# GateLoop and squared ReLU on one core: the inverse of the running products taken from 1/|a| and from each block's product, and idle products in every planned TensorE stop

## The chip, the core and the metric

The kernel runs on one core of one Trainium2 chip. A core has five engines that work side by side, each through its own queue in order: TensorE (PE) multiplies matrices into PSUM, VectorE (DVE) and ScalarE (ACT) do elementwise work, GpSimd (POOL) and SyncE (SP) here mostly issue DMA transfers. The metric is the device time of one execution in microseconds (us). The kernel before takes 721.93 us, the median of three runs (720.88 to 722.63).

## The reference

A gated linear recurrence with complex gates, for 4 batches, 8 heads, 768 positions and head size 48, followed by a two-layer block with squared ReLU on 3072 tokens (384 to 2048 to 384). All is fp32.

```python
mag = np.sqrt(a_re * a_re + a_im * a_im)
scale = np.minimum(mag, 0.999) / (mag + 1e-06)
a_re_n, a_im_n = (a_re * scale, a_im * scale)
for t in range(S):
    ar, ai = (a_re_n[:, :, t, :, None], a_im_n[:, :, t, :, None])
    new_re = ar * S_re - ai * S_im
    new_im = ar * S_im + ai * S_re
    kv = np.einsum('bhd,bhe->bhde', k[:, :, t], v[:, :, t])
    S_re, S_im = (new_re + kv, new_im)
    y[:, :, t] = np.einsum('bhd,bhde->bhe', q[:, :, t], S_re)
# y is regrouped to x: (B*S, H*D)
h = x @ w_in
r = np.maximum(h, 0.0)
out = (r * r) @ w_out
```

## The kernel before

The tokens are cut into six units of 512 (`n` = 0 to 5). Within a unit, partition p holds four consecutive steps (`c` = 0 to 3) of all eight heads, in two halves of four heads (`z` = 0, 1). A tile with one value per step, head and channel of a half is 128 x 768 fp32. A batch has 768 steps, so unit 1 and unit 4 cross from one batch to the next (`cross`), and units 2 and 5 end with a batch (`ends`).

Instead of stepping, the kernel multiplies queries by the running product of the gates and keys by its inverse, and then uses masked products of queries and keys. The inverse of a complex number is its conjugate over its squared size, so what is needed is one over the squared size of each running product. This is what the change touches. Per unit:

- `chain(n)`: `roots` computes 1/|a| (Ln, Exp with -0.5, one Newton step) into slot 3 (`t`) of the four slots `col[z]` of the buffer `f`. `normalise` makes from it the normalised gates: f0 = 0.999 t, f1 = 1 - 1e-6 t, gate times min(f0, 1) f1 (L938 to L945). `inner` forms the running products over the four steps in a partition (L964 to L972) and copies the last ones, the blocks' own products, to `xn[:, 0:2]` (L979). `totals`, `scan` and `back` form the running products over the 128 partitions: a turn on TensorE (L1023), small complex products on VectorE, a turn back, a copy by ACT (L1217). After `back`, `xn[:, 0:2]` is the running product ahead of each block.
- `inverse(z)`: squares of the running products in the partition (L984), their sum (L986), Ln (L988), Exp with -1 (L990) and a Newton step (L992, L994) give one over the squared size of all 768 values; the last of each four goes to `xn[:, 2]` (L999).
- `factors(lo, hi, rk)`: the same inverse for the products ahead of the blocks, by a running product of the blocks' inverses: TensorE turns `xn[:, 2]` (L1071), `scan_x` on VectorE runs six scans of 64 (L1092), starting from a small constant or from the value kept of the unit before (`cx`), and writes two checks of range (`grow`, L1096, and `total`, L1100); TensorE turns back (L1114), ACT copies (L1117). Unit 0 does it in two parts, one for each z.
- `twist(z)` multiplies the keys by the inverses in the partition (L1004). `apply(z, p, np)` multiplies the gates' running products by `xn[:, 0:2]` (L1255, L1259), the keys by `xn[:, 2]` (L1262), and queries and keys by the result (L1269). It uses the slots of `f` as its own buffers; from unit 2 on it does four heads at once, L1255's second half into slots 2 and 3.
- `gather` sends slices of the keys between partitions by DMA (L1309, to `KC`). `pairs(n)` turns queries and keys (`turn_pe` on TensorE in units 0 and 1, L1368 and L1372; `turn` by VectorE and DMA afterwards), forms scores (L1386), masks them (L1389), updates the state (L1414 to L1425) and mixes (L1438, L1442); ACT copies the output to `yt` (L1448) and a DMA takes it to `xT` (L1456).
- `dense(n, grp)` multiplies `xT` by the first weights (L1478), ACT squares the ReLU (L1509, L1510), and TensorE multiplies by the second weights (L1524 in unit 0, L1575 in `eight` and `seven` after that).

The weights arrive once, as 64-bit floats, and are converted in pieces on ACT and VectorE (L805 to L818) during units 0 and 1. `check` steps sum squares of inputs on ACT (L948, L952, L1228, L1231) into `sums`; `verdict` compares them, and a flag chooses a general path if they leave the range.

No order is written out by hand. Each helper hands a step (engine, estimated duration, what it reads and writes, a rank) to `Plan.add`. `Plan.order` builds the order of all engines by simulating them with these estimates: of the steps that are ready on an engine, it takes the one of the lowest rank, then the oldest. To a TensorE step's wait for another engine after 100 us it adds a margin of 0.6 us, and of 2.0 us where scores and state products wait for transfers. If TensorE stands for more than `FILL` = 1.0 us before a step, and the planned time is under `UNTIL` = 100 us, `Plan.emit` puts idle products ahead of it, `(stop - 0.3) / 0.22` of them: products of the identity with itself into bank `d2` (L711), read by nobody. The eight PSUM banks are `d0` to `d2` (dense products; in unit 0 `turn_pe` uses the first two), `sc0`, `sc1`, `tr0`, `tr1` (turns; in unit 1 `turn_pe`), and `yp`.

Of the kernel before, what the change touches and what calls it, by code (L numbers as in the profile page):

```python
# [480 lines left out]
class Plan:  # L481
# [7 lines left out]
    FILL, EACH, UNTIL = 1.0, 0.22, 100.0  # L489

    def __init__(self, idle):
        self.idle = idle
        self.steps = []
        self.wrote = {}
        self.read = {}

    def add(self, eng, dur, reads, writes, fn, rank, wire=None, group=None, after=(), slack=False):

        n = len(self.steps)
        deps = set(after)  # L500
# [18 lines left out]
    def order(self):  # L519
# [30 lines left out]
        for _ in steps:  # L550
# [46 lines left out]
def fast_path(ctx, tc, q, k, v, a_re, a_im, moe_w_in, moe_w_out, out, flag):  # L597
# [6 lines left out]
    C = 128  # L604
# [13 lines left out]
    CUT = C // 2  # L618
# [32 lines left out]
    x = sb("x", NM * (C + 1)).rearrange("p (m c) -> p m c", m=NM)  # L651
    xe = sb("xe", NM)
    txs = [sb(f"tx{j}", 3 * 24).rearrange("p (r g) -> p r g", r=3) for j in range(2)]
    ce = sb("ce", 2 * NM).rearrange("p (r m) -> p r m", r=2)
    cx = sb("cx", NM)
# [16 lines left out]
    NS = 10  # L672
    sums = sb("sums", NU * NS).rearrange("p (n j) -> p n j", n=NU)
    grow = sb("grow", NU * 2 * NM).rearrange("p (n j m) -> p n j m", n=NU, j=2)
    total = sb("total", B * NM).rearrange("p (b m) -> p b m", b=B)
# [27 lines left out]
    for t in txs:  # L703
        pool.memset(t, 0.0)
    pool.memset(good, 1.0)
    pool.memset(col, 1.0)
# [4 lines left out]
    plan = Plan(lambda: pe.matmul(bank["d2"][:, 0:C], lhsT=ident, rhs=ident, start=True,  # L711
                                  stop=True))
# [176 lines left out]
    def chain(n):  # L889
# [46 lines left out]
        def normalise(z):  # L936
            f0, f1, _, t = col[z]
            step("ACT", ac(Y), key(z, 3), key(z, 0), lambda: act.activation(  # L938
                out=f0, in_=t, func=AF.Copy, scale=0.999), first)
            step("ACT", ac(Y), key(z, 3), key(z, 1), lambda: act.activation(  # L940
                out=f1, in_=t, func=AF.Copy, scale=-1e-6, bias=1.0), first)
# [9 lines left out]
            if n == 0:  # L951
                check("ACT", ac(Y), key(z, 2), [], lambda: act.activation(  # L952
                    out=junk[:, 0:Y], in_=col[z][2], func=AF.Copy, saturate=False,
                    accum_out=sums[:, n, z:z + 1]), first)
# [26 lines left out]
        def inverse(z):  # L981
            f0, f1, d, t = col[z]
            rk = late[z]
            step("ACT", ac(Z), [("a", z)], key(z, 0, 1), lambda: act.activation(  # L984
                out=ff[z][:, 0:Z], in_=A[z], func=AF.Square), rk)
            step("DVE", tt(Y), key(z, 0, 1), key(z, 2), lambda: dve.tensor_tensor(  # L986
                out=d, in0=f0, in1=f1, op=ALU.add), rk)
            step("ACT", ac(Y), key(z, 2), key(z, 0), lambda: act.activation(  # L988
                out=f0, in_=d, func=AF.Ln), rk)
            step("ACT", ac(Y), key(z, 0), key(z, 1), lambda: act.activation(  # L990
                out=f1, in_=f0, func=AF.Exp, scale=-1.0), rk)
            step("DVE", tt(Y), key(z, 1, 2), key(z, 3), lambda: dve.scalar_tensor_tensor(  # L992
                out=t, in0=d, scalar=-1.0, in1=f1, op0=ALU.mult, op1=ALU.mult), rk)
# [767 lines left out]
```

## Time and profile before

| | us |
|---|---|
| median of three runs | 721.93 |
| profiled execution, whole | 722.42 |
| its span, first to last instruction | 720.6 |
| TensorE busy | 698.5 (97%) |
| VectorE busy | 576.5 (80%) |
| ScalarE busy | 358.7 (50%) |
| GpSimd busy | 176.3 (24%) |
| idle products L711 among TensorE's | 64.0, 530 records |
| TensorE's last product ends at | 713.9 |

A busy TensorE is not a useful one: the records of idle products count too. Each fp32 product leaves two records. Records of matmuls overlap, so the pace of a stream is read from the chain of waits (when a stretch starts and how long it takes), not from the mean of a record. A share of busy time is a mean over stages with different limits, so the stages are looked at one by one.

### The profile page before, as it was taken

How to read it: one execution, taken by the hardware profiler on the slowest of the kernel's cores; microseconds unless marked ns; L12 is line 12 of the kernel's file. 1: busy time of each engine (PE TensorE's matmuls, PEld its weight loads, DVE VectorE, ACT ScalarE, POOL GpSimd, SP SyncE). 2: the span in 40 equal slices, each digit the busy share in tenths (PEclk: the TensorE clock that was granted, in tenths of full speed). 3: DMA queues.
4: the chain of work that ended last, by engine and by line, in shares of the span. 5: the costliest groups of instructions: out<-in, count | busy, mean ns of one | idle time of the engine just before them, and what ended most of it. 6: DMA issues, size and time to landing. Idle time of an engine off the chain costs nothing.

```text
span 720.6 us, 12695 instructions
## 1 busy us (share of the span) xinstructions
PE 698.5 (97%) x4648; PEld 633.5 (88%) x4648; DVE 576.5 (80%) x1188; ACT 358.7 (50%) x579; POOL 176.3 (24%) x333
## 2 busy tenths in 40 slices
PE   9999889999988999999999999999999999999996
PEld 9998778677767898999999898998998989999995
DVE  6999999799777599889799588999788997347521
ACT  6693557975465713447713659324479142122230
POOL 6504253052400003314026040033050033032100
PEclk9999899999998999999999999999999999999998
DMA  9742359230530003645007671017560045197400
GB/s 284 213 161 53 79 117 288 81 66 18 162 107 23 1 12 98 176 112 155 1 25 200 158 150 40 0 55 196 136 162 4 10 122 132 47 356 238 152 2 26
DMA packets 56360, 79.60 MB, mean 110 GB/s; under 512 B 10944, under 2 KB 38464, under 8 KB 56288
## 3 DMA queue, kind: packets, MB, share of 16 engines
q0 software_dynamic: 15232, 40.72, 18.7%
q1 hardware_dynamic: 36928, 32.98, 18.0%
q10 hardware_dynamic: 4128, 4.98, 2.6%
q8 instruction: 39, 0.64, 0.4%
q14 instruction: 33, 0.27, 0.1%
HBM read 48.76 MB, written 4.72 MB: 74 GB/s over the span
## 4 chain that ended last, share of the span: by engine, by line
PE 81%; DVE 10%; ACT 3%; DMA 2%; SPq 1%; issue 1%; POOL 0%; DVEq 0%; ACTq 0%; POOLq 0%
PE d L1478 29%; PE d L1575 26%; PE d L711 7%; PE sc L1386 5%; PE d L1524 4%; PE tr L1414 3%; PE yp L1438 2%; PE yp L1442 2%; DVE f L964 2%; PE tr L1023 1%; DMA KC<-f 1%; SPq L1309 1%; DVE w L818 1%; PE tr L1071 1%; DVE aq L945 1%
## 5 line engine op out<-in xcount | busy, mean ns | idle before, releaser
L1478 PE MATMUL d<-xT,w 128*128 128x256 f32 x1056 | 236.2, 381 | 1.0 <-DMA xT<-yt 1.0
L1478 PEld LDWEIGHTS d<-xT,w 128*128 128x128 f32 x1056 | 199.2, 191 | 27.6 <-issue 1.1
L1575 PE MATMUL d<-w,g 128*128 128x192 f32 x768 | 132.3, 327 | 0.0
L1575 PEld LDWEIGHTS d<-w,g 128*128 128x128 f32 x768 | 124.9, 190 | 1.0 <-issue 0.7
L1509 ACT ACTIVATE g<-d 128x512 f32<-128x512 f32 x88 | 52.4, 595 | 127.5 <-PE d L1478 111.0
L1309 POOL DMA_DIRECT2D KC<-f x160 | 78.9, 501 | 117.2 <-DVE f L1269 55.9
L1590 DVE TENSOR_TENSOR g<-g 128x512 f32<-128x512 f32 x64 | 43.7, 689 | 37.1 <-ACT g L1510 21.5
L885 POOL DMA_DIRECT2D v<-in_v_dram x80 | 46.7, 590 | 86.5 <-PE yp L1438 30.3
L1575 PE MATMUL d<-T,g 128*128 128x192 f32 x384 | 66.8, 326 | 0.0
L711 PE MATMUL d<-ident 128*128 128x128 f32 x530 | 64.0, 283 | 1.5 <-POOL ident masks.py:199 1.5
L711 PEld LDWEIGHTS d<-ident 128*128 128x128 f32 x530 | 62.7, 199 | 1.8 <-POOL ident masks.py:199 1.5
L1575 PEld LDWEIGHTS d<-T,g 128*128 128x128 f32 x384 | 62.9, 190 | 0.0
L1536 POOL DMA_DIRECT2D out_dram<-ot x22 | 12.4, 563 | 206.4 <-DVE ot L1599 136.5
L1510 ACT ACTIVATE g<-g 128x512 f32<-128x512 f32 x96 | 60.6, 631 | 3.0
L1386 PE MATMUL sc<-QT 96*128 96x128 f32 x368 | 49.8, 291 | 4.2 <-ACT QT L1372 3.3
L1386 PEld LDWEIGHTS sc<-QT 96*128 96x128 f32 x368 | 46.0, 202 | 7.2 <-ACT QT L1372 4.1
L1269 DVE TENSOR_TENSOR f<-aq 128x384 f32<-128x384 f32 (+1 forms) x64 | 45.0, 752 | 0.6
L1255 DVE TENSOR_TENSOR f<-aq,xn 128x384 f32<-128x384 f32 (+1 forms) x64 | 44.7, 748 | 0.0
L1524 PE MATMUL d<-w,g 128*128 128x384 f32 x128 | 43.3, 488 | 0.7 <-DVE w L818 0.7
L1599 DVE TENSOR_TENSOR ot<-ot,d 128x192 f32<-128x192 f32 x64 | 21.7, 349 | 21.6 <-PE d L1575 21.1
L1448 ACT COPY yt<-yp 112x512 f32<-112x512 f32 x24 | 26.2, 1092 | 23.4 <-PE yp L1442 23.4
L964 DVE TENSOR_TENSOR f<-aq 128x384 f32<-128x384 f32 x72 | 36.9, 554 | 0.9
(196 smaller groups left out, 1029.7 us busy)
## 6 DMA issues: line engine op xcount, KB each, us to landing
QT<-aq SPq DMA_DIRECT2D x128, 64.0 KB, 2.0
f<-in_moe_w_in_dram POOLq DMA_DIRECT2D x8, 768.0 KB, 7.1
f<-in_moe_w_out_dram POOLq DMA_DIRECT2D x8, 768.0 KB, 5.9
KC<-f POOLq DMA_DIRECT2D x104, 48.0 KB, 2.6
out_dram<-ot POOLq DMA_DIRECT2D x22, 192.0 KB, 2.2
QT<-aq ACTq DMA_DIRECT2D x64, 64.0 KB, 2.3
v<-in_v_dram POOLq DMA_DIRECT2D x80, 48.0 KB, 2.9
xT<-yt SPq DMA_DIRECT2D x36, 96.0 KB, 2.4
```

What stands on the lines that cost most here:

```text
L711: plan = Plan(lambda: pe.matmul(bank["d2"][:, 0:C], lhsT=ident, rhs=ident, start=True, stop=True))
L885: lambda i=i, c=c, src=src: pool.dma_start(out=t[32 * c:32 * c + 32, i], in_=src[c]), vrank, 32 * 1536, 4.0,
L964: dve.tensor_tensor(out=f, in0=a[:, :, :, c - 1], in1=a[:, j, :, c].unsqueeze(1).to_broadcast([C, 2, HH, D]), op=ALU.mult)
L1255: lambda j=j, r=r: dve.tensor_tensor(out=f4[:, j, r], in0=a[:, r], in1=over(j), op=ALU.mult), late[z])
L1269: lambda j=j, r=r, o=o: dve.tensor_tensor(out=o[:, :, :, r * D:(r + 1) * D], in0=qk[:, j], in1=a[:, r], op=ALU.mult), late[z])
L1309: lambda i=i, c=c, queue=queue: queue.dma_start(out=kc[32 * c:32 * c + 32, i], in_=nat[32 * i:32 * i + 32, c]),
L1386: pe.matmul(sa[:, j], lhsT=T[:, j, 1, h], rhs=T[:, j, 0, h], start=True, stop=True)
L1478: pe.matmul(ps, lhsT=w1[:, f // FP, m, ts(f % FP, C)], rhs=xT[:, n % 2, m, ts(grp, G)], start=(m == 0), stop=(m == NM - 1))
L1509: act.activation(out=o, in_=ps, func=AF.Relu)
L1510: act.activation(out=o, in_=o, func=AF.Square)
L1524: pe.matmul(ps, lhsT=gt[:, f % 2, ts(i, C)], rhs=w2[:, f], start=(f == 0), stop=(f == NF - 1))
L1575: pe.matmul(bank[b][:, 0:DH], lhsT=g4[:, r, j], rhs=w(j), start=first and j == 0, stop=last and j == NT - 1)
```

## The change

`inverse` no longer squares the running products. In `normalise`, f1 is now made in two steps, f2 = 1 + 1e-6 t into slot 2 and f1 = 2 - f2; slot 2 is kept. `inverse` takes max(t, 1/0.999) times f2 for each single step, squares it, and multiplies along the four steps in the partition, three products of 192 elements for each half. The result stays in slot 2, where `twist` reads it. The unit-0 sum over slot 2 moves ahead of f2, which overwrites that slot.

`factors` is called once for a unit, with both halves, and takes the products ahead of the blocks, `xn[:, 0:2]`, after `back`: squares, a sum, a scaling where the sum is under 1, Ln, Exp with -1, a Newton step, all on 128 x 384, into `xn[:, 2]`. The turns, the scans and the carried value are gone. In units that cross or end a batch, two products of 192 and a sum on ACT write a new column of `sums`. A step `edges` squares 24 values of each part of `xn` for the check of range, which `verdict` evaluates.

In the planner, idle products fill stops over 0.8 us at any time, into a bank of `d2`, `d1`, `d0` that is free by the plan. `turn_pe` in unit 0 takes all three d banks in turn.

```diff
-    FILL, EACH, UNTIL = 1.0, 0.22, 100.0
-
-    def __init__(self, idle):
+    FILL, EACH = 0.8, 0.22
+
+    def __init__(self, idle, banks):
         self.idle = idle
+        self.lives = {b: [[]] for b in banks}
...
+        for k in {*reads, *writes}:
+            if k[0] in self.lives:
+                self.lives[k[0]][-1].append(n)
...
                 stop = t - free[e]
-                if t < self.UNTIL and stop > self.FILL:
-                    self.fill[n] = int((stop - 0.3) / self.EACH)
+                spare = [b for b in self.lives if self.spare(b, done, free[e])]
+                if spare and stop > self.FILL:
+                    self.fill[n] = int((stop - 0.3) / self.EACH), spare[0]
...
+    def spare(self, b, done, t):
+
+        return all(all(done.get(n, 1e9) < t - 0.5 for n in life) or not any(n in done for n in life)
+                   for life in self.lives[b])
+
     def emit(self):
         for n in self.order():
-            for _ in range(self.fill.get(n, 0)):
-                self.idle()
+            many, b = self.fill.get(n, (0, None))
+            for _ in range(many):
+                self.idle(b)
...
         def normalise(z):
-            f0, f1, _, t = col[z]
+            f0, f1, f2, t = col[z]
             step("ACT", ac(Y), key(z, 3), key(z, 0), lambda: act.activation(
                 out=f0, in_=t, func=AF.Copy, scale=0.999), first)
-            step("ACT", ac(Y), key(z, 3), key(z, 1), lambda: act.activation(
-                out=f1, in_=t, func=AF.Copy, scale=-1e-6, bias=1.0), first)
+            if n == 0:
+                check("ACT", ac(Y), key(z, 2), [], lambda: act.activation(
+                    out=junk[:, 0:Y], in_=f2, func=AF.Copy, saturate=False,
+                    accum_out=sums[:, n, z:z + 1]), first)
+
+            step("ACT", ac(Y), key(z, 3), key(z, 2), lambda: act.activation(
+                out=f2, in_=t, func=AF.Copy, scale=1e-6, bias=1.0), first)
+            step("ACT", ac(Y), key(z, 2), key(z, 1), lambda: act.activation(
+                out=f1, in_=f2, func=AF.Copy, scale=-1.0, bias=2.0), first)
             step("DVE", tt(Y), key(z, 0, 1), key(z, 0), lambda: dve.scalar_tensor_tensor(
                 out=f0, in0=f0, scalar=1.0, in1=f1, op0=ALU.min, op1=ALU.mult), first)
...
         def inverse(z):
-            f0, f1, d, t = col[z]
+
+
+            _, _, f2, t = col[z]
             rk = late[z]
-            step("ACT", ac(Z), [("a", z)], key(z, 0, 1), lambda: act.activation(
-                out=ff[z][:, 0:Z], in_=A[z], func=AF.Square), rk)
-            step("DVE", tt(Y), key(z, 0, 1), key(z, 2), lambda: dve.tensor_tensor(
-                out=d, in0=f0, in1=f1, op=ALU.add), rk)
-            step("ACT", ac(Y), key(z, 2), key(z, 0), lambda: act.activation(
-                out=f0, in_=d, func=AF.Ln), rk)
-            step("ACT", ac(Y), key(z, 0), key(z, 1), lambda: act.activation(
-                out=f1, in_=f0, func=AF.Exp, scale=-1.0), rk)
-            step("DVE", tt(Y), key(z, 1, 2), key(z, 3), lambda: dve.scalar_tensor_tensor(
-                out=t, in0=d, scalar=-1.0, in1=f1, op0=ALU.mult, op1=ALU.mult), rk)
-            step("DVE", tt(Y), key(z, 1, 3), key(z, 3), lambda: dve.scalar_tensor_tensor(
-                out=t, in0=t, scalar=2.0, in1=f1, op0=ALU.add, op1=ALU.mult), rk)
-            xh = xn.rearrange("p r (h d) -> p r h d", h=H)[:, :, ts(z, HH)]
-            t4 = t.rearrange("p (h c d) -> p h c d", h=HH, c=W)
-            step("ACT", ac(Y // W), key(z, 3), third(z * HH * D, (z + 1) * HH * D),
-                 lambda: act.copy(out=xh[:, 2], in_=t4[:, :, W - 1]), rk)
+            step("DVE", tt(Y), key(z, 2, 3), key(z, 2), lambda: dve.scalar_tensor_tensor(
+                out=f2, in0=t, scalar=1.0 / 0.999, in1=f2, op0=ALU.max, op1=ALU.mult), rk)
+            step("ACT", ac(Y), key(z, 2), key(z, 2), lambda: act.activation(
+                out=f2, in_=f2, func=AF.Square), rk)
+            t4 = f2.rearrange("p (h c d) -> p h c d", h=HH, c=W)
+            for c in range(1, W):
+                step("DVE", tt(Y // W), key(z, 2), key(z, 2), lambda c=c: dve.tensor_tensor(
+                    out=t4[:, :, c], in0=t4[:, :, c - 1], in1=t4[:, :, c], op=ALU.mult), rk)
 
         def twist(z):
-            t = col[z][3]
+            t = col[z][2]
             kk = QK[z][:, Y:2 * Y]
-            step("DVE", tt(Y), key(z, 3) + [("qk", z)], [("k", z)], lambda: dve.tensor_tensor(
+            step("DVE", tt(Y), key(z, 2) + [("qk", z)], [("k", z)], lambda: dve.tensor_tensor(
                 out=kk, in0=kk, in1=t, op=ALU.mult), late[z])
...
-        def factors(lo, hi, rk):
-
-            rows = [(m, max(lo - C * m, 0), min(hi - C * m, C)) for m in range(lo // C, (hi - 1) // C + 1)]
-            ks = third(lo, hi)
-            b = trs[slot["tr"] % 2]
-            ps = bank[b][:, 0:DM].rearrange("p (m t) -> p m t", m=NM)
-            slot["tr"] += 2
-
-            def go():
-                for m, p0, p1 in rows:
-                    pe.matmul(ps[p0:p1, m], lhsT=xn[:, 2, C * m + p0:C * m + p1], rhs=ident,
-                              start=True, stop=True)
-            step("PE", 0.12 * len(rows), ks, [(b,)], go, rk)
-
-            groups = [([m for m, p0, p1 in rows if (p0, p1) == (0, C)], 0, C)] + [
-                ([m], p0, p1) for m, p0, p1 in rows if (p0, p1) != (0, C)]
-
-            def scan_x():
-                for ms, p0, p1 in groups:
-                    if not ms:
-                        continue
-                    sl = slice(ms[0], ms[-1] + 1)
-                    if fresh:
-                        dve.memset(x[p0:p1, sl, 0], SCALE ** -2)
-                    else:
-                        dve.tensor_copy(out=x[p0:p1, sl, 0], in_=cx[p0:p1, sl])
-                    for hf in range(2):
-                        t0, t1 = hf * CUT, (hf + 1) * CUT
-                        if hf and cross:
-                            dve.memset(x[p0:p1, sl, t0], SCALE ** -2)
-                        for m in ms:
-                            dve.tensor_tensor_scan(
-                                out=x[p0:p1, m, t0 + 1:t1 + 1], data0=ps[p0:p1, m, t0:t1],
-                                data1=mask[p0:p1, 0:CUT], initial=x[p0:p1, m, t0:t0 + 1],
-                                op0=ALU.mult, op1=ALU.bypass)
-                        dve.scalar_tensor_tensor(
-                            out=grow[p0:p1, n, hf, sl], in0=x[p0:p1, sl, t0], scalar=2.0 ** 124,
-                            in1=x[p0:p1, sl, t1], op0=ALU.mult, op1=ALU.is_ge)
-                        if (ends and hf) or (cross and not hf):
-                            dve.tensor_scalar(
-                                out=total[p0:p1, ps_[0][2], sl], in0=x[p0:p1, sl, t1],
-                                scalar1=2.0 ** 114, scalar2=None, op0=ALU.is_le)
-                    if not ends:
-                        dve.tensor_copy(out=cx[p0:p1, sl], in_=x[p0:p1, sl, C])
-            kx = [("x", i) for _, _, i in ks]
-            check("DVE", sum(0.5 + 0.6 * len(ms) for ms, _, _ in groups if ms), [(b,)] + kx, kx,
-                  scan_x, rk)
-
-            b2 = trs[(slot["tr"] + 1) % 2]
-            ps2 = bank[b2][:, 0:DM]
-
-            def go2():
-                for m, p0, p1 in rows:
-                    pe.matmul(ps2[:, C * m + p0:C * m + p1], lhsT=x[p0:p1, m, 0:C],
-                              rhs=ident[p0:p1, p0:p1], start=True, stop=True)
-            step("PE", 0.12 * len(rows), kx, [(b2,)], go2, rk)
-            step("ACT", ac(hi - lo), [(b2,)], ks, lambda: act.copy(
-                out=xn[:, 2, lo:hi], in_=ps2[:, lo:hi]), rk)
+        def factors(rk):
+
+            X = [("xn", 2, i) for i in range(6)]
+            e0, e1, d = (e[:, j].rearrange("p w g -> p (w g)") for j in range(3))
+            f = x[:, 0:DM]
+            step("ACT", ac(2 * DM), [("xn", j, z) for j in range(2) for z in range(2)], E,
+                 lambda: act.activation(out=e[:, 0:2].rearrange("p r w g -> p r (w g)"),
+                                        in_=xn[:, 0:2], func=AF.Square), rk)
+
+            def scaled():
+
+                dve.tensor_tensor(out=d, in0=e0, in1=e1, op=ALU.add)
+                dve.tensor_scalar(out=f, in0=d, scalar1=1.0, scalar2=2.0 ** 59,
+                                  op0=ALU.is_lt, op1=ALU.mult)
+                dve.scalar_tensor_tensor(out=d, in0=f, scalar=2.0 ** -59, in1=d,
+                                         op0=ALU.max, op1=ALU.mult)
+            step("DVE", 2 * tt(DM) + ts2(DM), E, E + [("x",)], scaled, rk)
+            step("ACT", ac(DM), E, E, lambda: act.activation(out=e0, in_=d, func=AF.Ln), rk)
+            step("ACT", ac(DM), E, E, lambda: act.activation(
+                out=e0, in_=e0, func=AF.Exp, scale=-1.0), rk)
+
+            def refined():
+                dve.scalar_tensor_tensor(out=e1, in0=d, scalar=-1.0, in1=e0,
+                                         op0=ALU.mult, op1=ALU.mult)
+                dve.scalar_tensor_tensor(out=e1, in0=e1, scalar=2.0, in1=e0,
+                                         op0=ALU.add, op1=ALU.mult)
+                dve.scalar_tensor_tensor(out=xn[:, 2], in0=f, scalar=2.0 ** -59, in1=e1,
+                                         op0=ALU.max, op1=ALU.mult)
+            step("DVE", 3 * tt(DM), E + [("x",)], E + X, refined, rk)
+            if not ends and not cross:
+                return
+
+            for z in range(2):
+                t3 = col[z][2].rearrange("p (h c d) -> p h c d", h=HH, c=W)[:, :, W - 1]
+                step("DVE", tt(Y // W), key(z, 2) + X, [("x",)], lambda z=z, t3=t3:
+                     dve.tensor_tensor(
+                         out=x[:, ts(z, DM // 2)].rearrange("p (h d) -> p h d", h=HH),
+                         in0=t3, in1=xn[:, 2, ts(z, DM // 2)].rearrange(
+                             "p (h d) -> p h d", h=HH), op=ALU.mult), rk)
+            check("ACT", ac(DM), [("x",)], [], lambda: act.activation(
+                out=junk[:, 0:DM], in_=x[:, 0:DM], func=AF.Copy, saturate=False,
+                accum_out=sums[:, n, NS - 1:NS]), rk)
...
+        def edges(r):
+            blocks = xn[:, r].rearrange("p (g b) -> p g b", b=32)[:, :, ::31]
+            check("ACT", 0.2, [("xn", r, 0), ("xn", r, 1)], [], lambda: act.activation(
+                out=ends_of[:, n, r], in_=blocks, func=AF.Square), ahead)
...
+            edges(j)
...
-            factors(zs[0] * HH * D, (zs[-1] + 1) * HH * D, late[zs[0]])
+            if 0 in zs:
+                factors(rank)
...
+        if kind == "d":
+            plan.lives["d%d" % (s % n)].append([])
...
-                b = "d%d" % (take("d0", 2)) if n == 0 else trs[take("tr", 2)]
+                b = "d%d" % take("d", 3) if n == 0 else trs[take("tr", 2)]
...
-            for lo, hi, top_ in ((0, 2, 60), (2, 4, 12), (4, NS, 20)):
+            for lo, hi, top_ in ((0, 2, 60), (2, 4, 12), (4, NS - 1, 20), (NS - 1, NS, 114)):
...
-            dve.tensor_reduce(out=good[:, 1:2], in_=grow, axis=AXYZ, op=ALU.min)
-            dve.tensor_reduce(out=good[:, 2:3], in_=total, axis=AXY, op=ALU.min)
+            for b in range(2):
+                dve.tensor_tensor(out=ends_of[:, :, 0, :, b], in0=ends_of[:, :, 0, :, b],
+                                  in1=ends_of[:, :, 1, :, b], op=ALU.add)
+            grow = ends_of[:, :, 1, :, 0]
+            dve.scalar_tensor_tensor(out=grow, in0=ends_of[:, :, 0, :, 0], scalar=2.0 ** -124,
+                                     in1=ends_of[:, :, 0, :, 1], op0=ALU.mult, op1=ALU.is_le)
+            dve.tensor_reduce(out=good[:, 1:2], in_=grow, axis=AXY, op=ALU.min)
```

More of the change, by code (lines that the diff above doesn't have):

```diff
@@ L617, in fast_path @@
     G = L // 2
-    CUT = C // 2
     Z = 2 * HH * W * D
@@ L650, in fast_path @@
     el = sb("el", 3 * NM).rearrange("p (r m) -> p r m", r=3)
-    x = sb("x", NM * (C + 1)).rearrange("p (m c) -> p m c", m=NM)
-    xe = sb("xe", NM)
+    x = sb("x", DM)
     txs = [sb(f"tx{j}", 3 * 24).rearrange("p (r g) -> p r g", r=3) for j in range(2)]
     ce = sb("ce", 2 * NM).rearrange("p (r m) -> p r m", r=2)
-    cx = sb("cx", NM)
     xn = sb("xn", 3 * DM).rearrange("p (r n) -> p r n", r=3)
@@ L671, in fast_path @@
     mask = sb("mask", C)
-    NS = 10
+    NS = 11
     sums = sb("sums", NU * NS).rearrange("p (n j) -> p n j", n=NU)
-    grow = sb("grow", NU * 2 * NM).rearrange("p (n j m) -> p n j m", n=NU, j=2)
-    total = sb("total", B * NM).rearrange("p (b m) -> p b m", b=B)
+    ends_of = sb("ends_of", NU * 2 * NM * W * 2).rearrange("p (n r g b) -> p n r g b", n=NU,
+                                                           r=2, b=2)
     odd = sb("odd", NF)
@@ L705, in fast_path @@
     pool.memset(good, 1.0)
+    pool.memset(sums, 0.0)
     pool.memset(col, 1.0)
@@ L708, in fast_path @@
     pool.memset(txs[1].rearrange("p r (m k) -> p r m k", k=4)[:, 0, :, 0], 1.0)
-    plan = Plan(lambda: pe.matmul(bank["d2"][:, 0:C], lhsT=ident, rhs=ident, start=True,
-                                  stop=True))
+    plan = Plan(lambda b: pe.matmul(bank[b][:, 0:C], lhsT=ident, rhs=ident, start=True,
+                                    stop=True), ["d2", "d1", "d0"])
     def vs(n):
@@ L950, in normalise @@
                 accum_out=sums[:, n, 2 + z:3 + z]), first)
[L951 to L954, printed above, removed]
         def inner(z):
@@ L981, in inverse @@
         def inverse(z):
[L982 removed]
+            _, _, f2, t = col[z]
             rk = late[z]
[L984 to L999 removed]
+            step("DVE", tt(Y), key(z, 2, 3), key(z, 2), lambda: dve.scalar_tensor_tensor(
[6 more added lines that the diff above has]
+                    out=t4[:, :, c], in0=t4[:, :, c - 1], in1=t4[:, :, c], op=ALU.mult), rk)
         def twist(z):
[L1002 removed]
+            t = col[z][2]
             kk = QK[z][:, Y:2 * Y]
[L1004 removed]
+            step("DVE", tt(Y), key(z, 2) + [("qk", z)], [("k", z)], lambda: dve.tensor_tensor(
                 out=kk, in0=kk, in1=t, op=ALU.mult), late[z])
+        E = [("e", 0), ("e", 1), ("e", 2)]
         for fn in (roots, normalise, inner):
@@ L1142, in minus @@
             dve.tensor_scalar(out=ni, in0=im, scalar1=-1.0, scalar2=None, op0=ALU.mult)
-        E = [("e", 0), ("e", 1), ("e", 2)]
         I = [("yt", 0), ("yt", 1)]
@@ L1311, in gather @@
                     rank, 32 * w * 4, group=(n, p))
-    slot = {"d0": 0, "tr": 0, "sc": 0, "A": 0, "St": 0, "yt": 0, "QT": 0, "d": 0, "ot": 0, "g": 0}
+    slot = {"tr": 0, "sc": 0, "A": 0, "St": 0, "yt": 0, "QT": 0, "d": 0, "ot": 0, "g": 0}
     trs = ["tr0", "tr1"]
@@ L1666, in verdict @@
         ps = bank["tr0"][0:1, 0:1]
-        step("DVE", 2.2, [], [("good",)], collect, (LATE, 99), after=checked)
+        step("DVE", 2.6, [], [("good",)], collect, (LATE, 99), after=checked)
         step("PE", 0.3, [("good",)], [("tr0",)], lambda: pe.matmul(
```

## The prediction

> **What bounds the kernel now.** I read the slices first, then a table of busy time by stage, the chain of waits, the groups of instructions by shape, and the timeline where these left a question. All times are of the profiled execution: span 720.6 us, whole run 722.42 us, so 1.8 us lie around the span. The median of the runs is 721.93, half a microsecond lower. A difference under 0.2% (1.4 us) can't be told from none.
>
> The slices show TensorE near full throughout, but its clock below full in two slices before the last, and VectorE near full until slice 10:
>
> ```profile
> PE   9999889999988999999999999999999999999996
> ...
> DVE  6999999799777599889799588999788997347521
> ...
> PEclk9999899999998999999999999999999999999998
> ```
>
> The stages (columns: stretch, its length, then busy us of PE, weight loads, DVE, ACT, POOL; then the clock):
>
> ```profile
> 20.00:132.00 112.00, 105.57 (x834) 96.25 (x833) 106.45 (x239) 73.06 (x111) 39.15 (x69) 0.97 0.52 145
> 132.00:196.00 64.00, 63.87 (x312) 46.90 (x313) 54.47 (x134) 39.49 (x67) 23.42 (x44) 1.00 0.30 79
> 196.00:232.50 36.50, 31.50 (x234) 25.83 (x233) 27.55 (x45) 24.11 (x39) 0.57 (x1) 0.91 0.24 69
> ...
> 250.00:345.00 95.00, 95.00 (x660) 88.82 (x660) 83.56 (x168) 44.40 (x72) 23.26 (x44) 1.00 0.40 105
> ```
>
> Until 132 us TensorE's high share is mostly idle products (L711, below); the engine that works is VectorE, 106.45 of 112 us: unit 0's chain, the weight conversions, unit 1's start. VectorE then carries unit 1's chain until 196, and the last outputs of unit 1's pairs, with waits between TensorE, ACT and DMA, set the moment 232.5 at which `dense(1)` flows. From 250 to 713.9 TensorE does not stop: 95.00 of 95, and in later stages 102.00 of 102 and 99.21 of 100. So before about 232 us a saving must come out of VectorE or latency, after it out of TensorE.
>
> The chain of waits (start, us, what) shows the products that the change removes, in unit 2, with dense products straight after them; and one score step that takes twice its usual time:
>
> ```profile
> 182.03 1.78 PE sc L1386 x16
> ...
> 219.09 3.78 PE sc L1386 x16
> ...
> 267.49 0.67 PE tr L1071 x6
> 268.16 3.90 PE d L1575 x24
> 272.06 0.67 PE tr L1114 x6
> 272.73 16.84 PE d L1478 x78
> ```
>
> The same pair stands at 365.04/369.61, 469.63/475.50 and 570.25/576.12. The groups give the prices (after the first bar: total us, mean ns):
>
> ```profile
> L711 PE MATMUL d<-ident 128*128 128x128 f32 x530 | 64.0, 283 | 1.5 <-POOL ident masks.py:199 1.5
> ...
> L964 DVE TENSOR_TENSOR f<-aq 128x384 f32<-128x384 f32 x72 | 36.9, 554 | 0.9
> ...
> L970 DVE TENSOR_TENSOR aq<-f 128x192 f32<-128x192 f32 x36 | 12.8, 356 | 1.1
> ...
> L992 DVE SCALAR_TENSOR_TENSOR f<-f 128x768 f32<-128x768 f32 x12 | 11.4, 953 | 5.3 <-ACT f L990 5.3
> ```
>
> **What the skill says.** "VectorE: DVE Perf Modes", section on the TRN2 errata, prices an fp32 tensor_tensor at (N+151)/0.96 ns: 955 ns for N = 768, 557 for 384, 357 for 192. The three rows above agree. "TensorE: Matmul & The Clock Gate", section "What's actually happening", says that the array's clock falls to half after an idle window of about 3.4 us and returns after a busy one. The trace shows half speed (3.78 against 1.78 us), but behind shorter stops: 1.54 us before 217.0, 1.44 before 219.09. The same page, "Architectural detail", calls ACT and DVE strict FIFO queues; the order in the timeline fits that.
>
> **The change, part by part.**
>
> *Old inverse (L984 to L999) and scan (`factors`).* In each unit VectorE loses L986, L992 and L994, two each: 6 x 0.955 = 5.73 us. `scan_x` ran in the timeline at 53.48 to 55.71 and 77.40 to 80.39 in unit 0 (5.22 us with a wait of 0.65 for L1071), at 167.19 to 169.75 in unit 1 (2.56), at 268.72 to 270.94 in unit 2 (2.22).
>
> *New inverse and factors.* VectorE gains 2 x 0.955 for f2, 6 x 0.354 for the products over the four steps, five ops of 384 at 0.55, and one tensor_scalar of 384, which no row shows: between L838 (768: 0.57) and L1142 (96: 0.225) I take 0.37. Sum 1.91 + 2.12 + 2.75 + 0.37 = 7.15 us; in units 1, 2, 4 and 5 two more of 0.354.
> Unit 0: 5.73 + 5.22 - 7.15 = 3.8 us less. Unit 1: 5.73 + 2.56 - 7.86 = 0.4 less. Both lie where VectorE bounds, so I count 4.2. Units 2 to 5 save 0.1 to 0.8 of VectorE, beside a saturated TensorE: nothing.
>
> *ACT.* Per unit it loses 2 x 1.48, 2 x 0.845, 2 x 0.841, 2 x 0.346 and 0.476 = 7.5 us and gains about 5.5 to 6.2 (two more 768-wide ops in `normalise`, two squares, one square of 768, Ln and Exp of 384, `edges` at 0.2 each by the 3-element L1044, and in four units a 384-wide check). At half load this bounds nothing. But f1 now waits for f2: one ACT op more in the startup. L942 began at 15.62 with f1 out at 15.19; one more at 0.75 spacing puts it near 16.05: cost 0.4. Bounds: 0 if VectorE hides it, 1.2 if the moved unit-0 sum gets in front too. In unit 1 conversions cover it; in unit 2 it isn't on the way to 232.5.
>
> *TensorE.* L1071 and L1114 go: 2 x 0.67 = 1.34 us in each of units 2 to 5, 5.4 us in the saturated stage, all on the path. Unit 1's pair (166.02, 170.58) lies where VectorE sets the end: nothing, at best 1.3. Unit 0's lie among idle products. What is late next? The pairs' last transfers were issued by 324.3, 421.1, 526.9 and 627.1; with the 2.4 us that they take to land, `dense(2)` to `dense(5)` had 4.6 to 11 us of margin before 331.3, 434.6, 535.2 and 635.4. A gain of 1.34 a unit doesn't use it up.
>
> *The new wait.* The factor needed by L1262 hangs on `back(1)`, an ACT square, three DVE ops, Ln, Exp, three DVE ops. In unit 2: 268.0 + 0.9 + 1.5 + 1.2 + 1.6 = 273.2. Before, the path through L1071, scan, L1114 and L1117 ended at 273.3. Even. ACT's dense pairs (0.60 + 0.63) may stand in front twice: up to 2.4 us. Behind the waiting op on VectorE stand `twist` and L1255, 1.9 + 3.6 us that don't need it; in units 2, 4 and 5 half of L1255 now also waits, since the ending check reads the slot it writes. Gathers and pairs wait for those; the margin above holds them. If the cover fails in units 0 and 1, it costs the 4.2.
>
> *Idle products.* One takes 32.76/136 = 0.241 us (two records each), planned as 0.22. They now fill planned stops over 0.8 us everywhere. Gain: the slow clock at 219 to 227 cost 1.9 us on L1386 and 0.8 on twelve L1478 records (3.43 against 2.60), on the way to 232.5. Bounds 0 to 2.7; I take 1.2, as only stops that the planner foresees are filled. Cost: a fill ends 0.3 before the planned start less its own overrun of a tenth, while the plan adds 0.6 of margin to each cross-engine wait after 100 us; so a step really ready early is held some 0.3 us. Three to four such places on the path: 1.0, bounds 0 to 2.5. After 250 I take none. Rotating unit 0's transposes over three banks instead of two removes waits of 0.24 to 0.5 (61.62, 86.90) beside a busy VectorE: nothing. The larger `verdict` ran at 677 to 679, under TensorE's work.
>
> Sum: -4.2 + 0.4 - 5.4 - 1.2 + 1.0 = -9.4. From 722.4 this gives 713.0; the median's 0.5 is within the noise.
>
> **Rivals.**
> A. Only TensorE's saving arrives. The reordered queue or the ACT-DVE ping-pong in units 0 and 1 eats VectorE's 4.2: 722.4 - 5.4 + 0.4 = 717.4. For it: VectorE has long idle before L992 (5.09 us at 250.5) waiting for ACT, so ACT latency can reach it. Against it: until 132 conversions fill its gaps.
> B. More arrives: the cold stretch goes wholly (2.7), no fill holds anything, unit 1's TensorE pair counts: -4.2 + 0.4 - 5.4 - 2.7 - 1.3 = -13.2, 709.2.
> C. Slower: idle products in the saturated stage. The plan adds 0.6 us (2.0 before scores and state products) to waits that the chip doesn't have; where it therefore sees a stop over 0.8, products are put before work that was ready. Each place costs 2 to 7 products, 0.5 to 1.7 us, say 0.7. From 13 places after 250 us the gain is gone; four a unit over five units, 20, would be +14: about 727. For it: TensorE idles there under 1 us in all, so every product would be pure cost. Against: a stop caused by a 0.6 margin alone stays under 0.8, and dense products of the unit before usually stand ready.
>
> **How the numbers follow.** Main case 0.53, A 0.18, B 0.12, C 0.17. The main case's own range is 710.5 to 715.5. The range from 707 to 720 takes in A and B with their scatter of 2 us; C stays outside. Faster by over 0.2%: main, B, and nearly all of A, with a little of each lost to an unlucky order: 0.79. Within 0.2%: 0.05, where A and C overlap. Slower: 0.16.
>
> **What will show it.** No L1071 or L1114, and units following each other 1.3 us faster from 250 on; first dense stretch of `w2` products (132.13 before) about 3.4 us earlier; the start of steady flow (232.5) about 4 us earlier; no 3.78 us score step. Wrong if L711 records appear by dozens after 250 us (C), if the 132 moment stays (A), or if TensorE shows stops after 250 that wait for L1262's factor.

## The result and the profile after

| | before | after |
|---|---|---|
| median of the runs, us | 722.01 (720.88 to 722.63, 4 runs) | **2326.53** (2322.91 to 2327.40, 4 runs) |
| ratio | | **3.2231** [3.2164, 3.2299] |
| profiled execution, whole | 722.42 | 2326.07 |
| its span | 720.6 | 2324.4 |

The forecast was 713.0 in a range from 707 to 720. The kernel takes 1,604 us more than before. A change of a few microseconds in six units can't do that, so the first question is where the extra time lies, and the slices answer it (each digit is a fortieth of the span, here 58 us; tenths of busy time, and of the clock for PEclk):

```profile
span 2324.4 us, 61068 instructions
...
PE   9899999999991141467877877777787777787799
...
DVE  8998888989547999898788878968967969969840
...
PEclk9999999999995555578888888798788788797799
```

The span has two parts. The first twelve slices look like the kernel before: TensorE near full, at its clock. Then TensorE falls to a tenth, its clock to half, and another program runs. Busy time in three stretches of the kernel after (length, then PE, weight loads, DVE, ACT, POOL, the clock, the share of the DMA engines, GB/s) gives the border's two sides:

```profile
0.00:222.60 222.60, 209.50 (x1492) 179.60 (x1493) 197.96 (x413) 146.28 (x234) 75.46 (x147) 0.99 0.46 134
222.60:700.50 477.90, 473.71 (x3078) 440.97 (x3078) 374.57 (x757) 204.94 (x352) 101.14 (x187) 1.00 0.38 104
700.50:2324.40 1623.90, 1115.63 (x20840) 760.60 (x20840) 1291.92 (x2922) 379.38 (x857) 841.65 (x1115) 0.79 0.12 27
```

Up to 700.5 us there are 4,570 records of TensorE products; behind it 20,840. The timeline at the border shows what begins there (start, us, engine, line, operation; in brackets the idle time before and what ended it):

```profile
663.51 0.40 DVE L1656 TENSOR_SCALAR ok<-sums 128x12 f32<-128x12 f32 x4
...
671.93 0.14 DVE L1675 TENSOR_SCALAR flag<-tr 1x1 int32<-1x1 f32 x1 [0.73 <-PE tr L1673]
...
698.10 0.35 DVE L1599 TENSOR_TENSOR ot<-ot,d 128x192 f32<-128x192 f32 x1 [2.25 <-PE d L1575]
...
700.54 0.90 SPq L185 DMA_DIRECT2D a<-in_a_re_dram  x2
700.56 0.20 POOL masks.py:197 MEMSET ident<- 128x128 f32 x1 [40.49 <-DMA out_dram<-ot]
```

`verdict` compares the sums with their limits at 663.51 (L1656) and writes the flag at 671.93 (L1675). The last addition to an output is at 698.10. Then a load of the gates from L185 begins, at 700.54, when the answer is already in memory: the flag says that the inputs leave the range, and **the general path computes everything a second time**, in its own way, 1,623.9 us long. The groups of the kernel after name its work, complex products in a helper (L302) on GpSimd and VectorE:

```profile
L302 POOL TENSOR_TENSOR k<-K,T 128x384 f32<-128x384 f32 x384 | 421.3, 1113 | 143.3 <-DVE T L307 58.4
...
L302 DVE TENSOR_TENSOR q<-Q,T 128x384 f32<-128x384 f32 x448 | 292.5, 659 | 0.0
```

The fast part itself ended about 15 us sooner in this trace: its last addition is at 698.10, and in the trace of before at 713.57.

```profile
713.57 0.35 DVE L1599 TENSOR_TENSOR ot<-ot,d 128x192 f32<-128x192 f32 x1 [2.25 <-PE d L1575]
```

So there are two things to explain: why the flag goes up, and whether the gain in the fast part is what the prediction said.

**The theory on the flag.** Before, `total` compared each of a batch's 384 end values 1/|2^59 P|² with 2^114, each by itself (P is the product of a channel's 768 gates). The change sends the same values through an ACT sum over the 384, into the last column of `sums`, and that sum is compared with 2^114. The limit stayed; the quantity became up to 384 = 2^8.6 times as large. The reference's own inputs say what that means, in double precision:

```python
a = np.hypot(a_re, a_im)                      # float64
g = a * np.minimum(a, 0.999) / (a + 1e-6)
x = -118 - 2 * np.log2(g).sum(axis=2)         # log2 of 1/(2^59 |P|)^2
x = x.reshape(4, 384)
for r in x: print("%.2f %.2f" % (r.max(), np.log2(np.exp2(r).sum())))
```

```
111.50 113.86
109.42 113.54
111.19 113.98
111.61 114.43
```

The largest single value of each batch is at least 2.4 powers of two under the limit; three of the sums are just under it; the sum of the last batch, which unit 5 ends, is over it, by a factor of 2^0.43.

### The profile page after: what moved, and what is told of

Read it like the earlier page. It is cut to its first block, busy times and chain, and to the rows that moved or that the text cites. A ratio compares the mean times of both kernels' runs of the same rounds, so it can differ in the third digit from the quotient of the medians.

```text
span 2324.4 us, 61068 instructions
## 1 busy us (share of the span) xinstructions
PE 1798.8 (77%) x25410; PEld 1381.2 (59%) x25410; DVE 1864.4 (80%) x4091; ACT 730.6 (31%) x1443; POOL 1018.2 (44%) x1449
## 3 DMA queue, kind: packets, MB, share of 16 engines
q8 instruction: 201, 3.29, 0.6%
## 4 chain that ended last, share of the span: by engine, by line
DVE 50%; PE 37%; POOL 5%; ACT 4%; issue 3%; DMA 1%; DVEq 0%; SPq 0%; POOLq 0%; ACTq 0%
DVE q L302 9%; PE o L417 7%; PE d L1478 7%; PE d L1575 7%; DVE t L302 6%; DVE Q L305 4%; DVE Q L307 4%; DVE s L225 2%; PE h L407 2%; DVE A L264 2%; PE y L385 2%; DVE T L305 2%; PE y L390 2%; PE kv L353 2%; PE d L1524 2%
## 5 line engine op out<-in xcount | busy, mean ns | idle before, releaser
L302 POOL TENSOR_TENSOR k<-K,T 128x384 f32<-128x384 f32 x384 | 421.3, 1113 | 143.3 <-DVE T L307 58.4
L261 PE MATMUL lv<-Q,K 64*32 64x32 f32 x13824 | 178.7, 221 | 279.5 <-DVE Q L305 120.2
L261 PEld LDWEIGHTS lv<-Q,K 64*32 64x32 f32 x13824 | 155.4, 121 | 358.8 <-issue 145.6
L407 PE MATMUL h<-xT,w 128*128 128x384 f32 x768 | 349.1, 604 | 2.2 <-DVE xT L401 2.2
L302 DVE TENSOR_TENSOR q<-Q,T 128x384 f32<-128x384 f32 x448 | 292.5, 659 | 0.0
L417 PE MATMUL o<-w,g 128*128 128x384 f32 x768 | 280.1, 521 | 0.0
L407 PEld LDWEIGHTS h<-xT,w 128*128 128x128 f32 x768 | 167.9, 233 | 104.5 <-issue 44.5
L302 DVE TENSOR_TENSOR t<-T 128x384 f32<-128x384 f32 (+6 forms) x448 | 195.9, 470 | 0.0
L305 POOL TENSOR_TENSOR K<-k,k 128x192 f32<-128x192 f32 x192 | 136.4, 710 | 65.6 <-PE lv L279 60.1
L305 DVE TENSOR_TENSOR Q<-q,q 128x192 f32<-128x192 f32 x224 | 137.2, 612 | 1.1 <-PE lv L279 1.1
L307 POOL TENSOR_TENSOR K<-k,k 128x192 f32<-128x192 f32 x192 | 137.4, 715 | 0.0
L1575 PE MATMUL d<-w,g 128*128 128x192 f32 x768 | 131.9, 327 | 0.0
L307 DVE TENSOR_TENSOR Q<-q,q 128x192 f32<-128x192 f32 x224 | 129.4, 578 | 0.0
L1575 PEld LDWEIGHTS d<-w,g 128*128 128x128 f32 x768 | 124.9, 190 | 1.0 <-issue 0.7
```

The source lines that it names most:

```text
L261: nc.tensor.matmul(ps[ts(i, SB), h, ts(c, SB)], lhsT=u["K"][rows, j, cols], rhs=rhs, start=(j == 0), stop=(j == parts[-1]))
L302: eng.tensor_tensor(out=f, in0=x, in1=part, op=ALU.mult)
L305: eng.tensor_tensor(out=dst[:, 0], in0=ra[:, 0], in1=rb[:, 1], op=ALU.add if conj else ALU.subtract)
L307: eng.tensor_tensor(out=dst[:, 1], in0=ra[:, 1], in1=rb[:, 0], op=ALU.subtract if conj else ALU.add)
L407: nc.tensor.matmul(ps, lhsT=w1[:, m, ts(f, C)], rhs=g["xT"][:, m], start=(m == 0), stop=(m == NM - 1))
L417: nc.tensor.matmul(ps, lhsT=g["h"][f][:, ts(c, C)], rhs=w2[:, f], start=(f == 0), stop=(f == NF - 1))
```

## The experiments

Three theories were set against each other. S (sum): the column of end sums exceeds its limit in the last batch, and only that. O (other): another part of `verdict` raises the flag, such as the new test of growth within a block (`ends_of`), or a value of the new inverse that is wrong or not finite. P (path): the fast part itself is slower, and the flag has nothing to do with it. Beside them stood the sum of the prediction for the fast part.

**The limit raised to 2^116.** Nothing else is changed.

```diff
-            for lo, hi, top_ in ((0, 2, 60), (2, 4, 12), (4, NS - 1, 20), (NS - 1, NS, 114)):
+            for lo, hi, top_ in ((0, 2, 60), (2, 4, 12), (4, NS - 1, 20), (NS - 1, NS, 116)):
```

> The changed kernel with one number changed: the limit of the new column of sums, 2^116 in place of 2^114. Theory S (the sum over 384 channels is what raises the flag): from the reference's inputs the four sums work out at 2^113.86, 2^113.54, 2^113.98 and 2^114.43, so only the last batch's is over 2^114 and none is over 2^116; the general path stays away and the run takes what the trace of the changed kernel shows up to its last dense product, 698.4 us, plus 6.7 us of tail and 1.8 around the span: 707. Theory O (another part of the verdict raises it: the check on the block edges, or a value that is not finite): still about 2326. Theory P (the fast path itself is slower and the flag has nothing to do with it): over 722 and no instruction of the general path gone.

Measured: 708.36 us (706.77 to 708.92, 5 runs) against 721.97, ratio 0.9808 [0.9795, 0.9820]. The general path is gone, and the growth check, which this kernel keeps, raises nothing. One constant separates 2,326 us from 708.

**The limit kept, the last unit's sum not compared.**

```diff
+    pool.memset(ok, 1.0)
...
+                u = NU - 1 if lo == NS - 1 else NU
-                dve.tensor_scalar(out=ok[:, :, lo:hi], in0=sums[:, :, lo:hi],
+                dve.tensor_scalar(out=ok[:, 0:u, lo:hi], in0=sums[:, 0:u, lo:hi],
```

> The changed kernel with its limit of 2^114, but the verdict compares the new column for units 0 to 4 only; the range check of unit 5's last sum is left out. Theory S: only the last batch's sum is over the limit, so about 707. If several units' sums are over it, or theory O holds: about 2326.

Measured: 708.93 us (2 runs), ratio 0.9821 [0.9804, 0.9838]. With 2^114 in force for the other five units the flag stays down: it is the last batch's sum alone.

**The sum bracketed.** The same constant at 114.40 and at 114.45, on both sides of the 114.43 that was worked out.

> The changed kernel, limit of the new column 2^114.40. Theory S with the worked-out sum of 2^114.43 in the last batch: still over the limit, so the general path runs, about 2326. If the sum in the kernel were smaller, because its inverses or its summation are off: about 708.

> The changed kernel, limit 2^114.45. Theory S: the sum of 2^114.43 is now under the limit, about 708. If the sum in the kernel is larger than worked out: about 2326.

Measured: 2330.94 us and 707.16 us, one run each. The last batch's sum on the chip lies between 2^114.40 and 2^114.45, so it agrees with the one worked out to some 2%. A wrong value of the new inverse is therefore not what lifts it over the limit.

**Before, with its own limit lowered.** If the price is that of the general path and not of the change, the kernel before must pay it as well once one of its values leaves the range.

```diff
-                                scalar1=2.0 ** 114, scalar2=None, op0=ALU.is_le)
+                                scalar1=2.0 ** 111.5, scalar2=None, op0=ALU.is_le)
```

> The kernel before with its own limit on each channel's total lowered from 2^114 to 2^111.5. The largest single channel works out at 2^111.61 (last batch), 2^111.50 or less in the others. Theory S (before, the limit was put to the largest of 384 values, 2.4 powers of two under it, not to their sum): the flag goes up here too and the time is 722 plus the general path, which took 2326.5 - 707 = 1620 behind the changed kernel: about 2342. If the old quantity is something else, far below 2^111: 722.

Measured: 2334.58 us against 721.45, 1,613 more, one run. The general path costs 1,613 to 1,624 us (2330.94 less 707.16), whichever kernel stands ahead of it. That settles S against O and P: a changed limit alone moves the flag, in both kernels.

**Only the planner's part, in the kernel before**: idle products wherever TensorE is to stand over 0.8 us, on whichever of three banks is free, and unit 0's turns over three banks. The inverse stays as it was.

```diff
...
-                if t < self.UNTIL and stop > self.FILL:
-                    self.fill[n] = int((stop - 0.3) / self.EACH)
+                spare = [b for b in self.lives if self.spare(b, done, free[e])]
+                if spare and stop > self.FILL:
+                    self.fill[n] = int((stop - 0.3) / self.EACH), spare[0]
...
-                b = "d%d" % (take("d0", 2)) if n == 0 else trs[take("tr", 2)]
+                b = "d%d" % take("d", 3) if n == 0 else trs[take("tr", 2)]
```

> The kernel before with the planner's part of the change alone: idle products in every planned stop over 0.8 us, into a free bank, and unit 0's turns over three banks; the old inverse and scan stay. Theory F (idle products in later stops are worth something): 719 to 721. Theory N (they are worth nothing, since the changed kernel's trace shows only 12 of 528 records of idle products after 100 us, 6 of them after 132 us): 721 to 723. Rival C of the prediction (they cost): 724 or more.

Measured: 722.02 us (14 runs), ratio 1.0000 [0.9989, 1.0012]. No gain, although the fills (the idle products) speed up the products behind them. The timeline of TensorE in this kernel:

```profile
218.92 1.35 PE L722 MATMUL d<-ident 128*128 128x128 f32 x10
220.29 2.05 PE L1399 MATMUL sc<-QT 96*128 96x128 f32 x16
...
222.48 2.82 PE L1491 MATMUL d<-xT,w 128*128 128x256 f32 x12
...
232.54 7.11 PE L1491 MATMUL d<-xT,w 128*128 128x256 f32 x24 [1.91 <-DMA xT<-yt]
```

The score step takes 2.05 us where it took 3.78, and the twelve dense records 2.82 where they took 3.43. But the path goes on through ACT, which copies the unit's last outputs to `yt` for the transfer to `xT`. The copy and the start of the flow in the kernel before:

```profile
228.38 1.11 ACT L1448 COPY yt<-yp 112x512 f32<-112x512 f32 x1 [0.67 <-PE yp L1442]
...
232.54 5.42 PE L1478 MATMUL d<-xT,w 128*128 128x256 f32 x24 [0.56 <-DMA xT<-yt]
```

and the copy with the planner's part alone:

```profile
226.75 0.83 ACT L951 ACTIVATE f<-f 128x768 f32<-128x768 f32 x1
227.48 0.83 ACT L959 ACTIVATE junk<-f 128x768 fp8e5<-128x768 f32 x1
228.21 0.19 ACT L959 ACTIVATION_READ_ACCUMULATOR junk<-f 128x1 f32 x1
228.31 1.09 ACT L1461 COPY yt<-yp 112x512 f32<-112x512 f32 x1
```

Before, ACT stood waiting for the cold products. Here they end 1.4 us sooner, but the copy stands in ACT's queue behind work of the next unit, one step of which (the sum of L959) followed the copy before (L948), and it begins at the same time. So the transfer lands no sooner: TensorE waits 1.91 us for `xT`, and the flow (the steady run of `dense(1)`) starts at 232.54, the same as before to a hundredth. Behind this stop the clock falls. The granted clock (before the last two columns) is 0.72 between 232 and 238 us where it was 1.00, and 24 records take 7.11 us in place of 5.42:

```profile
232.00:238.00 6.00, 5.46 (x18) 4.55 (x19) 5.69 (x9) 1.27 (x3) 0.00 (x0) 0.72 0.01 3
```

The cold stretch has moved, it has not gone. A faster product is worth nothing where the copy behind it comes late anyway.

**Only the inverse, the planner's part left as before**, with the limit at 2^116.

```diff
-    FILL, EACH = 0.8, 0.22
+    FILL, EACH, UNTIL = 1.0, 0.22, 100.0
...
-                spare = [b for b in self.lives if self.spare(b, done, free[e])]
-                if spare and stop > self.FILL:
-                    self.fill[n] = int((stop - 0.3) / self.EACH), spare[0]
+                if t < self.UNTIL and stop > self.FILL:
+                    self.fill[n] = int((stop - 0.3) / self.EACH), "d2"
...
```

> The changed kernel with the limit 2^116 and the planner's part of before: idle products only before 100 us and over 1.0 us, into d2, and unit 0's turns over two banks. If the whole gain is the new inverse: 706 to 709, as with the limit alone. If the idle products carry the part of the gain between 132 and 232 us (6.8 us more than the 3.1 until 132): 712 to 715.

Measured: 710.89 us (710.13 to 713.68), ratio 0.9846 [0.9834, 0.9859]. That lies between the two ranges that were expected. So the inverse is worth 11.1 us, and the planner's part, worth nothing alone, 2.5 more beside it (708.36; the two intervals don't touch). The timelines show the half-speed stretch left in this kernel, and gone with the fills. The inverse alone:

```profile
212.21 0.64 PE L1367 MATMUL tr<-ident,f 128*96 128x128 f32 x4 [1.44 <-ACT QT L1371]
212.69 0.88 PE L1413 MATMUL tr<-T,KC 128*96 128x48 f32 x8
214.51 3.29 PE L1385 MATMUL sc<-QT 96*128 96x128 f32 x16 [0.94 <-ACT QT L1371]
...
218.16 3.75 PE L1477 MATMUL d<-xT,w 128*128 128x256 f32 x8
...
227.94 5.42 PE L1477 MATMUL d<-xT,w 128*128 128x256 f32 x24
```

And the kernel with the limit at 2^116, which has both:

```profile
212.75 0.90 PE L721 MATMUL d<-ident 128*128 128x128 f32 x6
213.48 1.95 PE L1386 MATMUL sc<-QT 96*128 96x128 f32 x16
...
215.57 1.96 PE L1478 MATMUL d<-xT,w 128*128 128x256 f32 x8
...
224.22 5.42 PE L1478 MATMUL d<-xT,w 128*128 128x256 f32 x24 [0.50 <-DMA xT<-yt]
```

Score and dense products take 3.29 + 3.75 = 7.04 us without the fills and 1.95 + 1.96 = 3.91 with them, 3.1 us less, and the score starts 1.0 us sooner. Of this 3.7 us are left at the start of the flow (227.94 to 224.22). In the kernel with the inverse alone TensorE runs from the score into the flow without a stop, so its own products are the path. With the fills, the transfer is the last to come again (0.50 us).

**The products of the turns put back**, as two groups of three idle products in each of units 2 to 5, at the place in the chain where `factors` begins; limit 2^116.

```diff
+            for b in trs if n > 1 else ():
+                def again(b=b):
+                    for m in range(NM):
+                        pe.matmul(bank[b][:, ts(m, C)], lhsT=ident, rhs=ident, start=True,
+                                  stop=True)
+                step("PE", 0.12 * NM, [("xn", 1, 0), ("xn", 1, 1)], [(b,)], again, rk)
...
```

> The changed kernel with limit 2^116, and in units 2 to 5 two groups of three idle products put back where the turns for the old scan stood. If TensorE bounds units 2 to 5, as the prediction says: 4 units x 2 x 0.67 = 5.4 more than with the limit alone, up to 5.8 by the idle product's own pace (0.241 us each, 24 of them): 713.8 to 714.2. If they are hidden: 708.4.

Measured: 713.0 us (709.74 to 713.38), ratio 0.9857 [0.9832, 0.9882]. The interval doesn't touch that of the kernel without them. In the traces the last group of the second weights' products (sixteen records; L1575, here L1581) starts 477.00 us after the flow (222.62 to 699.62), against 472.71 without them (224.22 to 696.93): 4.3 us for 24 products, somewhat under the 5.4 to 5.8 that were expected. The starts of that group, in the kernel before, with the limit at 2^116, and with the products put back:

```profile
710.76 2.76 PE L1575 MATMUL d<-T,g 128*128 128x192 f32 x16
...
696.93 2.76 PE L1575 MATMUL d<-T,g 128*128 128x192 f32 x16
...
699.62 2.76 PE L1581 MATMUL d<-T,g 128*128 128x192 f32 x16
```

In this stage products cost time even when nobody reads them.

**Unit 0's turns over two banks again**, fills as changed, limit 2^116.

> The changed kernel with limit 2^116 and the new idle products, but unit 0's turns over two banks as before. With the old idle products as well it took 710.89, with both new ones 708.36. If the idle products carry these 2.5 us: 708.4. If the third bank carries them: 710.9.

Measured: 709.87 us (708.83 to 711.66), ratio 0.9824 [0.9802, 0.9846]. It lies between the kernel with the whole change and that with the inverse alone, and its interval touches both: which part of the planner's 2.5 us belongs to the third bank isn't settled.

**The largest in place of the sum**, the limit at 2^114 as it was. VectorE takes the maximum over the 384 values into the same column.

```diff
-            check("ACT", ac(DM), [("x",)], [], lambda: act.activation(
-                out=junk[:, 0:DM], in_=x[:, 0:DM], func=AF.Copy, saturate=False,
-                accum_out=sums[:, n, NS - 1:NS]), rk)
+            check("DVE", tt(DM), [("x",)], [], lambda: dve.tensor_reduce(
+                out=sums[:, n, NS - 1:NS], in_=x[:, 0:DM], axis=AX, op=ALU.max), rk)
```

> The changed kernel with its limit of 2^114, but the column holds the largest of the 384 values (a maximum on VectorE, about 0.55 us in four units) instead of their sum (ACT). This is the quantity that the kernel before compared. Theory S: no general path, and the time of the limit alone within the noise, 708 to 709, as VectorE has room in units 2 to 5 and 0.55 us in unit 1. If VectorE's queue in unit 1 is on the path: up to 709.5.

Measured: **707.71 us** (705.62 to 709.81), ratio 0.9786 [0.9763, 0.9808]. It tests what the kernel before tested, each channel against 2^114, and is faster than the kernels before and after; from the one with the limit at 2^116 it can't be told apart. What the maximum makes of a value that is not a number was not tried.

## Why the prediction was wrong

**The step that failed** is the half sentence "The larger `verdict` ran at 677 to 679, under TensorE's work". It took `verdict` for a piece of work and asked when it runs; it never asked what it answers. The diff shows both halves of the matter, a sum over 384 values and the old limit of 2^114, and the reference gives the values. The runs show in its place a flag that goes up, on the last batch's sum of 2^114.43, and a general path of 1,613 to 1,624 us behind it. No rival said that the flag could go up, so the chance of slower, 0.16, stood on idle products alone. The one rival on that side, C, is refuted: the planner's part alone measures 1.0000 [0.9989, 1.0012], and no idle product (L722) runs after 260 us in it.

The price was not in the profile of before, because there the path wasn't taken. A rough estimate was possible: the general path does the whole computation again, so if it is no quicker than the fast one, a flag that goes up at least doubles the time of 722 us.

**The fast part, step by step**, from the kernel with the limit at 2^116 (708.36 against 721.97, so -13.6 in medians; predicted -9.4):

| term | predicted | measured |
|---|---|---|
| products of the turns, units 2 to 5 | -5.4 | -5.5: flow to last group 478.22 before, 472.71; -4.0 with the inverse alone (474.18); putting them back returns 4.3 |
| VectorE in units 0 and 1, with the later start | -3.8 | -4.6 at the start of the flow, inverse alone (232.54 to 227.94), for all that the inverse changes ahead of it |
| idle products: gain and cost together | -0.2 | -2.5 in medians beside the new inverse, 0.0 beside the old |

The traces of before and of the limit at 2^116 give -8.3 at the start of the flow and -5.5 behind it, together -13.8, beside -13.6 in medians. How the 8.3 divides is less certain. The start of the flow moves from trace to trace: 222.61, 224.22 and 225.06 in three kernels that are the same up to `verdict` but for a constant or a comparison. And the trace of the inverse alone is of the slowest of its five runs (713.68, median 710.89). So the first two terms have about the right size, the second for reasons that were not separated. The third was mis-sized: its gain was taken as 1.2 of a possible 2.7, and beside the new inverse the score and dense products alone give 3.1, while beside the old one nothing reaches the flow. The cost of 1.0 for steps held back was not isolated by any run. In sum the fast part came out as rival B, 709.2, had it, inside the forecast's range but below the main case's own (710.5 to 715.5). That the sum agrees doesn't show B's reasons: its term for unit 1's turns, 1.3, was not tested.

A slip of no weight: the formula that the prediction quotes gives 957 ns for 768 elements, not 955; the line measured 953.

*ACT's startup.* The first factor of VectorE (L942 before, L959 now) was put near 16.05. It starts at 16.09:

```profile
16.09 0.96 DVE L959 SCALAR_TENSOR_TENSOR f<-f 128x768 f32<-128x768 f32 x1 [0.39 <-ACT f L957]
```

*The first dense stretch of the second weights.* It was to start 3.4 us before 132.13. In kernels that are the same up to `verdict` but for a constant or a comparison it starts at 129.04, 129.57 and 131.56, so 0.6 to 3.1 sooner. VectorE is as busy there as before; for the kernel with the limit at 2^116, the windows of before's table:

```profile
20.00:132.00 112.00, 102.42 (x805) 93.53 (x805) 106.79 (x227) 73.55 (x114) 39.99 (x70) 0.97 0.53 147
132.00:196.00 64.00, 62.56 (x341) 46.74 (x341) 55.84 (x134) 39.90 (x72) 22.73 (x43) 1.00 0.33 91
...
250.00:345.00 95.00, 95.00 (x647) 88.28 (x646) 83.38 (x166) 51.06 (x89) 23.27 (x44) 1.00 0.39 105
```

VectorE's 106.79 us stand beside 106.45 before, so the room that the scans leave is taken by other work in its queue, and the stretch starts only a little sooner. The larger gain is seen at the start of the flow. In the last row TensorE is full as before, with 13 records fewer.

*The new wait.* The path from ACT's copy after the turn (L1213) to the factor in `xn` (L1095) was called even with the old one, some 5.3 us. In unit 2 of the same kernel:

```profile
257.44 0.48 ACT L1213 COPY xn<-tr 128x384 f32<-128x384 f32 x1 [1.15 <-PE tr L1031]
257.95 0.84 ACT L1075 ACTIVATE e<-xn 128x768 f32<-128x768 f32 x1
...
260.57 0.53 ACT L1086 ACTIVATE e<-e 128x384 f32<-128x384 f32 x1 [1.77 <-DVE e L1083]
261.13 0.53 ACT L1087 ACTIVATE e<-e 128x384 f32<-128x384 f32 x1
...
262.88 0.56 DVE L1095 SCALAR_TENSOR_TENSOR xn<-x,e 128x384 f32<-128x384 f32 x1
```

From 257.92 to 263.44 it is 5.5 us, with TensorE full beside it. TensorE's waits between 240 and 700 us come to 1.7 us in all (1.9 before), and none is for this factor. That step held.

## What to carry to other kernels

Before a change of a guard is priced, work out on which side of it the inputs fall: here the guard's own operations on VectorE take about 2 us, under TensorE's work, and what it chooses takes 1,620. When a test of each value becomes a test of their sum, or the other way, the limit has to be derived again (a sum of n values may reach n times the old limit), or the test has to stay a maximum. A saving on a busy engine may not show where the operation stood: here, with the whole change, the first dense stretch of the second weights came 0.6 to 3.1 us sooner, and the flow behind it 7.5 to 9.9. And when a product is made faster, look at the queue of the engine that copies its result.

## What was not expected of the hardware

- TensorE's clock fell to half after short stops. The Trainium skill ("TensorE: Matmul & The Clock Gate", section "What's actually happening") speaks of an idle window of about 3.4 us. In the kernel with the inverse alone, two stops of 1.44 and 0.94 us with 1.4 us of products between them were enough (score 3.29 us in place of 1.95), as 1.54 and 1.44 were in the kernel before. With the planner's part alone, a single stop of 1.91 us was enough (7.11 us in place of 5.42). The measurement decides: here no stop was as long as that window. Where the limit lies was not measured. With three idle products (six records, 0.90 us) in the place of the last stop and dense products in the place of the first, the clock stayed whole.
- The same planner's part was worth 0.0 in one kernel and 2.5 us in the other, though it cured the cold score step in both. What came next on the path differed: in the first ACT's copy, which began at 228.31 in place of 228.38, in the second TensorE's own products.
